# Bucketed attention and an MLP on one core: head pairs of the second pass transposed on TensorE instead of by DMA, four shared PSUM banks, scores in halves of 384 keys

## The chip, the core and the metric

The kernel runs on one core of a Trainium2 chip. A core has five engines with queues of their own: PE (TensorE, matrix products; its weight loads are listed as PEld), DVE (VectorE), ACT (ScalarE), POOL (GpSimd) and SP (SyncE, which here only issues DMA transfers). They share the on-chip memory SBUF (128 partitions); PE writes its products to PSUM, eight banks of 512 float32 words per partition, which DVE and ACT read and POOL does not touch in this kernel. The metric is the device time of one execution in microseconds, smaller is better.

## The reference, cut to what matters

The shapes are q, k, v of 4 batches x 8 heads x 768 rows x 64; proj is 64 x 6, w_in 512 x 2048, w_out 2048 x 512.

```python
q_bits = (np.einsum('bhsd,dk->bhsk', q, proj) > 0)      # k_bits alike
mask = q_bucket[:, :, :, None] == k_bucket[:, :, None, :]
scores = scale * np.matmul(q, k.transpose(0, 1, 3, 2))
scores = np.where(mask, scores, -1000000000.0)
attn = softmax(scores)                                  # minus the row's maximum; sum + 1e-9
x = np.matmul(attn, v)                                  # heads side by side: 3072 x 512
h = x @ w_in
out = (0.5 * h * (1.0 + erf(h / sqrt(2)))) @ w_out
```

A query sees only the keys whose six sign bits (the bucket) equal its own.

## The kernel before

**Number forms.** The MLP's products and most of the weighted sums of V are made of float16 halves: a number is written as a high and a low float16, and a product as three (high-high, high-low, low-high). Scores and hash are made in a 4-byte reduced form (`fp32r`), q and k each as a rounded part (tiles Aq, Ak) and a rest (Bq, Bk). The bits of query and key sit in extra rows of Aq and Ak, so that the score product itself lowers every pair of different buckets by a large number.

**A unit** is one head's 128 queries against all 768 keys; there are 192. `unit` (L688) plans it: the score product on PE (L697, L698) into a double bank `s`; the row's maximum on DVE (L701); two tiny DVE instructions (L705, L710); the exponential with its sum on ACT (L713) into `p`; a reciprocal (L722). Then the weights must be turned, keys to partitions, for the sum over V. That is done in one of two ways:

- *In halves* (all passes but the first): the weights times the reciprocal are written as a high float16 half `hl` on ACT, DVE or POOL (`affine`, L376 or L379), the low half by DVE (L728), and one transposing DMA turns both into `pt` (L735). The sum over V (L828) is then 36 float16 products for a pair of heads and 256 queries (a pair-chunk). V itself is split too (`values_halves`, L583).
- *Whole* (the first pass): a diagonal matrix `dr` with the reciprocals is made (L376/L379), PE multiplies the float32 weights with it, six 128x128 products that both scale and turn (L769, `whole_turn`), into two banks, and ACT or DVE copies each bank's 384 words to `pt`. The sum over V is 12 float32 products (L819), each of which leaves two records in the trace.

**Heads.** `head` (L594) loads a head's q and k, rounds them (Aq), moves halves (by DMA or an engine), subtracts for the rests (L398), makes the hash on PE (L659 to L664), its sign on ACT (L667), and the mask rows.

**Passes.** Pass one: batch 0, the first 256 queries of all eight heads (16 units). Pass two: batch 0, the other 512 queries in two chunks of 256, heads in reverse order (32 units). Then batches 1 to 3 with 48 units each. The number `cl` (0 for pass one, 1 for pass two, 2 after) chooses a pass's parameters and, before the change, whether weights are turned whole.

**The MLP** follows behind for each chunk of 256 rows, in two groups: the hidden layer (L1006) into `hp` banks, ACT copies it scaled (L1016), GELU, a split into halves `g` (one buffer), the output product (L1073), which adds up over both groups in the two banks `acc`, and a drain by DVE (L1093). The weights w_in and w_out are loaded, decoded by three integer instructions of DVE for each half (L452, L457, L462), scaled and split during passes one and two. The first output product waits for all of w_out.

**What sets the order.** The class `Plan` simulates the engines with a cost for every step, and each engine's queue is written in the order in which the simulation started its steps; ready steps of an engine compete by a key, which is the unit's number plus an offset from the table `PAR`. A step that can run on several engines takes the one that is free first. MLP steps have late keys (1000 and more) and so fill PE where attention leaves it free. Buffers are rings: a step that takes one waits until it is free. PSUM has the rings `s` (2 of two banks), `hp` (2 banks: hash, hidden layer, sum over V, weight statistics) and `acc` (2 banks: output sums, and under the name `turn` the whole turns of pass one).

Of the kernel before, what the change touches and what calls it, by code (L numbers as in the profile page):

```python
# [26 lines left out]
KEEP = 3  # L27
TABLE = 1.3
# [3 lines left out]
PAR = dict(H0=180.41, HL=-26.83, VS=-317.44, G2=1.83, HQ=-29.88, VQ=-3.01, in0=-31.49, out0=593.98, in1=111.61, out1=-36.62, in2=-95.35, out2=88.33, in3=-121.74, out3=193.55, H1=83.9, H2=30.05, H3=-106.39, H4=-26.07, H5=122.48, H6=11.83, H7=-6.57, MEV=-10, MGE=-10, MSP=-9, V0=74.23, QK0=76.28, QK1=22.19, QK2=79.24, MX0=-14.69, MX1=-2, MX2=67.11, EX0=-26.96, EX1=10.58, EX2=76.78, NR0=8.86, NR1=-1.85, NR2=92.39, HI0=-6.87, HI1=-39, HI2=-59.82, LO0=-16.45, LO1=50.99, LO2=34.82, PV0=94.26, PV1=48.91, PV2=24.55, TR0=-62.99, TR1=24.83, TR2=-50.58, V1=-109.62, V2=-89.25, Sin0=21.37, Sin1=-27.13, Sin2=50.05, Sin3=-25.72, Sout0=1.71, Sout1=35.63, Sout2=78.23, Sout3=-107.51, Lin=-90.3, Pin=-5.44, Qin=-44.82, Cin=-51.27, Min=-30.56, Lout=-67.78, Pout=75.58, Qout=-91.18, Cout=-17.92, Mout=204.75, G0=-24.93, G1=-27.5, G3=22.31, G4=-43.56, G5=-42.96, G6=-61.41, G7=2.72, DUP0=-47.65, DUP1=-23.1, DUP2=29.36, LOW0=-18.36, LOW1=24.39, LOW2=11.14, PRJ0=-0.65, PRJ1=-0.28, PRJ2=89.76, MSK0=66.33, MSK1=-99.41, MSK2=63.64, DI_ACT=-97.24, DI_DVE=-5.22, DI_Pool=0, WS_ACT=59.06, WS_DVE=0, WS_Pool=0, WH_ACT=-0.64, WH_DVE=0, WH_Pool=0, WL_ACT=0, WL_DVE=0.39, WL_Pool=0, VH_ACT=-74.31, VH_DVE=0.03, VH_Pool=0, MV_SP=0, MV_ACT=0, MV_DVE=0, MV_Pool=0, LO_ACT=0, LO_DVE=-37.1, LO_Pool=-1.97, RND_ACT=-0.17, RND_DVE=0, RND_Pool=0, MSK_ACT=-5.39, MSK_DVE=0, MSK_Pool=0, HI_ACT=-44.01, HI_DVE=0, HI_Pool=-3.05, DG_ACT=0.26, DG_DVE=0, DG_Pool=12.19, EV_ACT=0, EV_DVE=15.46, EV_Pool=0, GH_ACT=82.19, GH_DVE=-7.55, GH_Pool=52.8)  # L32
# [18 lines left out]
class Plan:  # L51
# [13 lines left out]
    START = {"DVE": 9.8, "Pool": 1.3, "SP": 0.7, "ACT": 3.7}  # L65
# [149 lines left out]
def tile_bucket_attention_moe(  # L215
# [33 lines left out]
        "s": 2, "hp": 2, "acc": 2, "p": 2, "hl": 2, "raw": 1, "rawe": RAWE, "sign": 1, "dr": 2, "turn": 2, "pt": NTH + 1,  # L249
# [5 lines left out]
    def ring(pool, name, shape, dtype, count, first=0):  # L255
# [48 lines left out]
    bufs["dr"] = ring(early, "dr", [P, P], F32, rings["dr"])  # L304
    bufs["turn"] = bufs["acc"]
# [15 lines left out]

    ident = const.tile([P, P], BF16, tag="ident", name="ident")
# [5 lines left out]
    off = const.tile([P, 1], F32, tag="off", name="off")  # L328
    nc.scalar.dma_start(out=off, in_=offset)
    praw = const.tile([P, 2 * NBIT], F32, tag="praw", name="praw")  # L330
    nc.scalar.dma_start(out=praw[:D, :NBIT], in_=proj)
    nc.scalar.dma_start(out=praw[D:, :NBIT], in_=proj)

    hash_hi = const.tile([P, D + P], F32R, tag="hash_hi", name="hash_hi")
    hash_lo = const.tile([P, P], F32R, tag="hash_lo", name="hash_lo")
    nc.vector.memset(hash_hi.bitcast(F32), 0.0)
    nc.vector.memset(hash_lo.bitcast(F32), 0.0)
    nc.vector.tensor_scalar(
        out=praw[:, NBIT:], in0=praw[:, :NBIT], scalar1=-1.0, scalar2=None, op0=ALU.mult
    )  # L340
    nc.vector.tensor_copy(out=hash_hi[:, D : D + 2 * NBIT], in_=praw)
    for rr in (slice(0, D), slice(D, P)):
        nc.vector.tensor_tensor(
            out=hash_lo[rr, rr.start : rr.start + 2 * NBIT], in0=praw[rr],
            in1=hash_hi[rr, D : D + 2 * NBIT].bitcast(F32), op=ALU.subtract,
        )
# [59 lines left out]
    def everywhere(t, top, key):  # L406
# [16 lines left out]
        return sc  # L423

# [169 lines left out]
    def head(b, h, i, key, clear, qr, cl):  # L594
# [57 lines left out]
        for c0, c1 in ((0, TC), (TC, S)):  # L652
# [4 lines left out]
            def project(n=n, box=box, with_q=with_q):  # L657
                pp = buf(box[0])[:, : n.stop - n.start]
                nc.tensor.matmul(pp, hash_lo, aq[:, n], start=True, stop=False)  # L659
# [12 lines left out]
            box.append(add("PE", 0.05 + (0.42e-3 * (2 + with_q)) * (c1 - c0), project, key + PAR[f"PRJ{cl}"], [space], takes="hp"))  # L672
# [15 lines left out]
    def unit(t, i, q0, qs, cl, made, place):  # L688
# [4 lines left out]

        def scores():
            for lo in range(0, S, 512):
                n = slice(lo, min(lo + 512, S))
                nc.tensor.matmul(buf(sp)[:, n], aq[:, qs], ak[:, n], start=True, stop=False)  # L697
                nc.tensor.matmul(buf(sp)[:, n], bq[:, qs.start - q0 : qs.stop - q0], bk[:, n], start=False, stop=True)  # L698
# [50 lines left out]
        if not cl:  # L749
            return sp, whole_turn(ex, nr, r, place, t)  # L750
# [9 lines left out]
    def whole_turn(ex, nr, r, place, t):  # L760
# [20 lines left out]
        dg = add(affine_on("DG", P, True), 0, diagonal, t + PAR["HI0"], [nr], takes="dr", port=True)  # L781
        prods, copies = [], []
        for n, (k0, k1) in enumerate(((0, KT // 2), (KT // 2, KT))):
            step = []
            step.append(
                add("PE", 0.214 * (k1 - k0), lambda k0=k0, k1=k1, step=step: product(k0, k1, step), t + PAR["LO0"], [dg], takes="turn")
# [4 lines left out]
                t + PAR["TR0"], [step[0], *hold[:1]], takes=None if hold else "pt",  # L791
# [10 lines left out]
    def values(b, pr, ch, vhl, turns, holds, key):  # L802
# [8 lines left out]

        whole = (b, ch) == (0, FIRST[0][0])
# [23 lines left out]
        for n, kt in enumerate(range(0, KT, 2)):  # L836
# [3 lines left out]
                    "PE", (0.9 if whole else 0.8) * nt / TC, lambda kts=kts: product(kts), key, [vh, vl, xt[b, ch], *turns, *parts],  # L840
# [311 lines left out]
```

## Time and profile before

| | |
|---|---|
| median of 3 runs | 972.09 us (970.51 to 973.16) |
| profiled execution | 971.92 us, span 970.1 us |
| PE busy | 874.6 us |
| DVE busy | 740.0 us |
| ACT busy | 640.9 us |
| POOL busy | 288.8 us |
| mean granted PE clock | 0.957 |

The busy time of an engine is the time in which it has an instruction running, as a sum over the span. In the rows of groups stand the line, engine, operation, output and inputs, shapes and count, then the busy time in us, the mean of one in ns, and the idle time before them with what ended it. The granted clock is the share of full speed at which PE was allowed to run.

### The profile page before, as it was taken

What the parts mean: (1) busy time and instruction counts of PE and PEld (TensorE: products, weight loads), DVE (VectorE), ACT (ScalarE), POOL (GpSimd) and SP (SyncE); (2) the same over time, 40 slices, a digit from 0 to 9 for tenths busy, and PEclk for the clock granted to TensorE, in tenths of its full rate; (3) what the DMA queues carried; (4) which work ended last, traced back from release to release, by engine and by line L of the source; (5) the groups of instructions that cost most, each with busy time, mean ns of one, the idle gap of its engine ahead of it and who ended that gap; (6) DMA issues with size and microseconds to landing.
All of it is one profiled execution on the core that took longest, in us unless ns stands there. A gap on an engine that the chain in (4) does not pass through costs nothing.

```text
span 970.1 us, 17419 instructions
## 1 busy us (share of the span) xinstructions
PE 874.6 (90%) x6512; PEld 630.8 (65%) x6512; DVE 740.0 (76%) x1607; ACT 640.9 (66%) x997; POOL 288.8 (30%) x241
## 2 busy tenths in 40 slices
PE   3768877556899999999999999999999999999998
PEld 2556666334576766867776676776776776667763
DVE  7888799999998879998897998998988842232222
ACT  4686788676868867888777778878878633112220
POOL 2565642722533224343232222423344100000000
PEclk9999888786799999999999999999999999999999
DMA  8654369786888778968677889876887830000000
GB/s 236 188 184 131 91 134 219 162 196 150 175 167 162 153 117 215 181 141 153 144 143 125 164 179 168 160 156 137 188 139 142 153 67 22 1 22 23 1 22 22
DMA packets 337124, 129.33 MB, mean 133 GB/s; under 512 B 278736, under 2 KB 322768, under 8 KB 337040
## 3 DMA queue, kind: packets, MB, share of 16 engines
q1 hardware_dynamic: 336736, 128.22, 62.6%
q8 instruction: 51, 0.84, 0.4%
q14 instruction: 33, 0.27, 0.1%
q10 hardware_dynamic: 304, 0.00, 0.0%
HBM read 45.49 MB, written 6.29 MB: 53 GB/s over the span
## 4 chain that ended last, share of the span: by engine, by line
PE 46%; DVE 14%; ACT 8%; DMA 7%; issue 4%; POOL 0%; SPq 0%; ACTq 0%; POOLq 0%; DVEq 0%
PE acc L1073 18%; PE hp L1006 16%; DMA pt<-hl 5%; PE hp L828 4%; PE s L697 4%; DVE rows L701 3%; PE s L698 3%; DVE hl L728 3%; ACT p L713 2%; DVE wraw L728 2%; DMA pt<-wraw 1%; DVE g L1054 1%; ACT h L1040 1%; ACT hl L376 1%; ACT L713 1%
## 5 line engine op out<-in xcount | busy, mean ns | idle before, releaser
L1006 PE MATMUL hp<-x,Win 128*128 128x256 f16 x2304 | 269.4, 274 | 0.4 <-ACT sign L667 0.4
L1073 PE MATMUL acc<-Wout,g 128*128 128x512 f16 x1152 | 261.0, 380 | 0.0
L1006 PEld LDWEIGHTS <-Win 128*128 128x128 f16 x2304 | 220.6, 98 | 35.1 <-issue 4.1
L701 DVE TENSOR_REDUCE rows<-s 128x1 f32<-128x768 f32 x192 | 179.8, 950 | 18.7 <-PE s L698 17.3
L1073 PEld LDWEIGHTS <-g 128*128 128x128 f16 x1152 | 108.0, 98 | 126.0 <-issue 5.1
L713 ACT ACTIVATE p<-s,rows 128x768 f32<-128x768 f32 x142 | 140.1, 987 | 45.1 <-DVE rows L710 17.0
L697 PE MATMUL s<-Ak,Aq 128*128 128x512 f32 x352 | 141.4, 404 | 27.4 <-ACT p L713 21.2
L1016 ACT ACTIVATE h<-hp,ffs 128x512 f32<-128x512 f32 x96 | 65.6, 683 | 133.2 <-PE hp L1006 132.8
L698 PE MATMUL s<-Bk,Bq 128*128 128x512 f32 x352 | 117.2, 353 | 0.0
L379 DVE TENSOR_SCALAR g<-h,ffs 128x512 f16<-128x512 f32 x48 | 25.0, 524 | 110.7 <-ACT h L1040 80.8
L697 PEld LDWEIGHTS s<-Ak,Aq 128*128 128x128 f32 x352 | 70.3, 200 | 60.0 <-ACT p L713 33.1
L728 DVE SCALAR_TENSOR_TENSOR hl<-p,rows,hl 128x768 f16<-128x768 f32 x95 | 103.3, 1095 | 7.2 <-ACT hl L376 6.2
L828 PE MATMUL hp<-pt,vhl 128*64 128x256 f16 x1584 | 100.8, 281 | 0.2 <-DVE x L855 0.2
L828 PEld LDWEIGHTS <-vhl 128*64 128x64 f16 x1584 | 84.7, 113 | 13.5 <-issue 7.8
L1054 DVE SCALAR_TENSOR_TENSOR g<-h,ffs,g 128x512 f16<-128x512 f32 x96 | 77.7, 816 | 14.6 <-ACT g L376 9.5
L698 PEld LDWEIGHTS s<-Bk,Bq 128*128 128x128 f32 x352 | 71.1, 202 | 9.7
L376 ACT ACTIVATE hl<-p,rows 128x768 f16<-128x768 f32 x53 | 49.1, 930 | 28.7 <-DMA pt<-hl 22.5
L667 ACT ACTIVATE sign<-hp,off 128x256 f32<-128x256 f32 (+1 forms) x74 | 42.0, 576 | 19.5 <-PE hp L664 19.0
L713 ACT ACTIVATE wraw<-s,rows 128x768 f32<-128x768 f32 x50 | 49.3, 986 | 7.2 <-DVE rows L710 4.5
L398 POOL TENSOR_TENSOR Bq<-raw,Aq 64x768 fp32r<-64x768 f32 (+1 forms) x22 | 41.2, 1871 | 39.6 <-ACT Aq L376 25.1
L379 POOL TENSOR_SCALAR hl<-p,rows 128x768 f16<-128x768 f32 x28 | 30.9, 1102 | 64.4 <-DVE rows L722 21.4
L1040 ACT ACTIVATE h<-h 128x2048 f32<-128x2048 f32 x24 | 45.9, 1911 | 0.4
(154 smaller groups left out, 1211.1 us busy)
## 6 DMA issues: line engine op xcount, KB each, us to landing
raw<-qk SPq DMA_DIRECT2D x29, 384.0 KB, 3.6
vraw<-v SPq DMA_DIRECT2D x28, 384.0 KB, 3.9
wraw<-w_in SPq DMA_DIRECT2D x16, 512.0 KB, 4.4
wraw<-w_out SPq DMA_DIRECT2D x16, 512.0 KB, 5.1
out<-o SPq DMA_DIRECT2D x12, 512.0 KB, 3.0
rawe<-qk SPq DMA_DIRECT2D x8, 384.0 KB, 3.2
Ak<-Aq SPq DMA_DIRECT2D x13, 192.0 KB, 4.0
Bk<-Aq SPq DMA_DIRECT2D x12, 192.0 KB, 3.2
```

Of the source, the lines that this page charges most:

```text
L376: nc.scalar.activation(out=out, in_=in_, func=AF.Copy, scale=scale, bias=bias)
L379: on.tensor_scalar(out=out, in0=in_, scalar1=scale, scalar2=bias, op0=ALU.mult, op1=ALU.add)
L697: nc.tensor.matmul(buf(sp)[:, n], aq[:, qs], ak[:, n], start=True, stop=False)
L698: nc.tensor.matmul(buf(sp)[:, n], bq[:, qs.start - q0 : qs.stop - q0], bk[:, n], start=False, stop=True)
L701: nc.vector.tensor_reduce(out=nm, in_=buf(sp)[:, :S], axis=AX.X, op=ALU.max, negate=True)
L713: nc.scalar.activation(out=buf(ex), in_=buf(sp)[:, :S], func=AF.Exp, scale=sc, bias=nb, accum_out=ssum)
L728: nc.vector.scalar_tensor_tensor(out=buf(hi)[:, 1], in0=buf(ex), scalar=r, in1=buf(hi)[:, 0], op0=ALU.mult, op1=ALU.subtract,)
L828: nc.tensor.matmul(pv[j * D : (j + 1) * D], buf(vh)[:, tv, kt, j * D : (j + 1) * D], buf(holds[j][0])[:, tp * KT + kt, :nt], start=kt == 0 ...
L1006: nc.tensor.matmul(buf(pair[0])[:, j * ch[1] : (j + 1) * ch[1]], win_hl[:, f0 // WB1, tw, pr, f0 % WB1 : f0 % WB1 + P], x[:, tx, pr, : ch[1]],
L1016: nc.scalar.activation(out=bufs["h"][0][:, 2 * fp : 2 * fp + 2, :nt], in_=buf(pair[0])[:, : 2 * nt].rearrange("p (j k) -> p j k", j=2), fu ...
L1054: nc.vector.scalar_tensor_tensor(out=gt[:, 1, s2, :nt], in0=h[:, s2, :nt], scalar=sg, in1=gt[:, 0, s2, :nt], op0=ALU.mult, op1=ALU.subtract,)
L1073: nc.tensor.matmul(bufs["acc"][u].rearrange("p (c f) -> p c f", c=NWB), gt[:, tg, f, u * P : (u + 1) * P], wout_hl[:, :, tw, ft], start=ft ...
```

## The change

It does six things.

1. `WHOLE = (4, 3, 0, 0, 0)` says how many head pairs of each pass turn their weights whole. Pass one keeps its four; in pass two the first three of four now do, 24 units of 32; `whole` takes the place of `not cl` in `unit` and `values`.
2. The rings `hp`, `acc` and `turn` become one ring `hp` of four PSUM banks. A chunk's output sums take two of them from the moment when the first split of its `g` is done until their drain.
3. The score product is made in two halves of 384 keys, each in a PSUM bank of its own, instead of 512 and 256; the maximum and the exponential read both as one two-part access.
4. The hash operand is 44 columns wide instead of 128, the keys' bits start at row 32, and the sign tile has 64 rows.
5. At the start, proj is loaded first, by one transfer on ACT's queue and one on SP's, ahead of the first head; the offset comes in two small transfers; `ones` is cleared on POOL, and four of the five Ak tiles are cleared by steps of the plan, on DVE or POOL.
6. The table `PAR`, some costs and a start time of the plan have new numbers, so the order moves everywhere.

```diff
+WHOLE = (4, 3, 0, 0, 0)
...
-        "s": 2, "hp": 2, "acc": 2, "p": 2, "hl": 2, "raw": 1, "rawe": RAWE, "sign": 1, "dr": 2, "turn": 2, "pt": NTH + 1,
+        "s": 2, "hp": 4, "p": 2, "hl": 2, "raw": 1, "rawe": RAWE, "sign": 1, "dr": 2, "pt": NTH + 1,
...
+    nc.scalar.dma_start(out=praw[:D, :NBIT], in_=proj)
+    nc.sync.dma_start(out=praw[D:, :NBIT], in_=proj)
...
-    nc.vector.memset(ones, 1.0)
-    for _, ak, _, _ in sets:
-        nc.vector.memset(ak[D:].bitcast(F32), 0.0)
...
+    nc.gpsimd.memset(ones, 1.0)
...
+    nc.vector.memset(sets[0][1][D:].bitcast(F32), 0.0)
...
+    cleared = {}
+    for n, (_, ak, _, _) in enumerate(sets[1:]):
+        box = []
+
+        def clear(ak=ak, box=box):
+            on = nc.vector if box[0].engine == "DVE" else nc.gpsimd
+            on.memset(ak[D:].bitcast(F32), 0.0)
+
+        box.append(add({"DVE": (0.7, 0.0), "Pool": (0.85, 0.0)}, 0, clear, n + PAR["Z"]))
+        cleared[n + 1] = box
...
+        def both(step):
+
+            return buf(step).rearrange("p (b k) -> p b k", b=2)[:, :, : S // 2]
+
         def scores():
-            for lo in range(0, S, 512):
-                n = slice(lo, min(lo + 512, S))
...
+            for half in range(2):
+                n = slice(half * S // 2, (half + 1) * S // 2)
+                to = both(sp)[:, half]
...
-        if not cl:
-            return sp, whole_turn(ex, nr, r, place, t)
+        if whole:
+            return sp, whole_turn(ex, nr, r, place, cl, t)
...
-                add("PE", 0.214 * (k1 - k0), lambda k0=k0, k1=k1, step=step: product(k0, k1, step), t + PAR["LO0"], [dg], takes="turn")
+                add("PE", 0.214 * (k1 - k0), lambda k0=k0, k1=k1, step=step: product(k0, k1, step), t + PAR[f"LO{cl}"], [dg], takes="hp")
...
-        whole = (b, ch) == (0, FIRST[0][0])
...
-                vhl = values_halves(b, pr, key, v_ready[b]) if cl else values_whole(b, pr, key)
+                whole = pos // 2 < WHOLE[n_pass]
+                vhl = values_whole(b, pr, key) if whole else values_halves(b, pr, key, v_ready[b])
...
+            banks = [add("none", 0, lambda: None, LATE + n, [cur["split"][0][1]], takes="hp") for u in range(nt // P)]
...
-            needs = [*cur["split"][f // 2], *acc[-1:]]
+            needs = [*cur["split"][f // 2], *acc[-1:], *banks]
             if g == 0 and f == 0:
-                needs += out_w if n == 0 else [drained]
+                needs += out_w if n == 0 else []
...
+            for bank in banks:
+                free(bank, [drained])
```

Counted over the whole program, the order has 240 of the 128x128 products with a diagonal instead of 96 (each a pair of records), 101 transposing transfers instead of 125, 152 low halves of weights on DVE instead of 176, 13 of V instead of 16, and 80 copies of turned weights out of PSUM instead of 32, 42 of them on DVE and 38 on ACT.

The order moves at the following places. In the rows stand the line of the kernel that they belong to, the operation, and output and inputs; hp, s, p, dr, pt and the others are the tiles named above, with a buffer's number behind them.

PE in pass two, before the change, around the 34th unit: scores of one unit follow those of another, and the hash of a later head (hash_lo, hash_hi) stands between them.

```order
L697 MATMUL s_61<-Ak_91,Aq_90 128x512
L698 MATMUL s_61<-Bk_93,Bq_92 128x512
L697 MATMUL s_61<-Ak_91,Aq_90 128x256
L698 MATMUL s_61<-Bk_93,Bq_92 128x256
L659 MATMUL hp_64<-x_105,hash_lo 128x256
L664 MATMUL hp_64<-x_107,hash_hi 128x256
L697 MATMUL s_62<-Ak_91,Aq_90 128x512
L698 MATMUL s_62<-Bk_93,Bq_92 128x512
L697 MATMUL s_62<-Ak_91,Aq_90 128x256
L698 MATMUL s_62<-Bk_93,Bq_92 128x256
```

PE at about the same place with the change:

```order
L788 MATMUL hp_64<-dr_120,p_68 128x128 x3
L788 MATMUL hp_65<-dr_119,p_67 128x128 x3
L788 MATMUL hp_66<-dr_119,p_67 128x128 x3
L715 MATMUL s_62<-Ak_91,Aq_90 128x384
L716 MATMUL s_62<-Bk_93,Bq_92 128x384
L715 MATMUL s_62<-Ak_91,Aq_90 128x384
L716 MATMUL s_62<-Bk_93,Bq_92 128x384
```

Products with the diagonal, three to a bank, now stand between the scores of one unit and the next, and take turns on the same four banks as all else.

DVE in pass two, before the change, around the 39th unit:

```order
L701 TENSOR_REDUCE rows<-s_62 128x1
L701 TENSOR_REDUCE rows<-s_61 128x1
L705 TENSOR_SCALAR rows<-rows 128x1
L728 SCALAR_TENSOR_TENSOR hl_70<-p_68,rows,hl_70 128x768
L710 TENSOR_SCALAR rows<-rows 128x1
L705 TENSOR_SCALAR rows<-rows 128x1
L462 SCALAR_TENSOR_TENSOR Wout<-wraw_82,Wout 128x512
L710 TENSOR_SCALAR rows<-rows 128x1
L462 SCALAR_TENSOR_TENSOR Wout<-wraw_83,Wout 128x512
L728 SCALAR_TENSOR_TENSOR hl_69<-p_67,rows,hl_69 128x768
```

DVE at about the same place with the change:

```order
L470 SCALAR_TENSOR_TENSOR Wout<-wraw_82,Wout 128x512
L470 SCALAR_TENSOR_TENSOR Wout<-wraw_81,Wout 128x512
L719 TENSOR_REDUCE rows<-s_62 128x1
L380 TENSOR_SCALAR pt_73<-hp_65 128x3x128
L723 TENSOR_SCALAR rows<-rows 128x1
L380 TENSOR_SCALAR pt_73<-hp_64 128x3x128
L728 TENSOR_SCALAR rows<-rows 128x1
```

The low halves are gone from between the maxima and the decodes of w_out, and copies of 384 words out of PSUM stand there.

DVE at the start, before the change:

```order
L325 MEMSET ones 128x128
L327 MEMSET Ak_87 64x768
L327 MEMSET Ak_91 64x768
L327 MEMSET x_106 64x768
L327 MEMSET Ak_112 64x768
L327 MEMSET Ak_116 64x768
L336 MEMSET hash_hi 128x192
L337 MEMSET hash_lo 128x128
L338 TENSOR_SCALAR praw<-praw 128x6
L341 CAST hash_hi<-praw 128x12
```

DVE at the start, with the change:

```order
L336 MEMSET hash_hi 128x76
L337 MEMSET hash_lo 128x44
L338 MEMSET Ak_87 64x768
L339 TENSOR_SCALAR praw<-praw 128x6
L342 CAST hash_hi<-praw 128x12
L344 TENSOR_TENSOR hash_lo<-praw,hash_hi 64x12 x2
L399 TENSOR_TENSOR Bq_88<-rawe_121,Aq_86 64x256
L399 TENSOR_TENSOR Bk_89<-rawe_121,Aq_86 64x768
```

Five of DVE's clearing instructions went to POOL's queue, and the rests of the first head came onto DVE. The first output product stands behind the 55th unit's scores, where it stood behind the 53rd; the hidden layer of the first chunk, which stood between the 20th and the 31st unit, is spread from the 22nd to the 47th.

More of the change, by code (lines that the diff above doesn't have):

```diff
@@ L64 @@
     SAME = {"PE": 0.0, "DVE": 0.13}
-    START = {"DVE": 9.8, "Pool": 1.3, "SP": 0.7, "ACT": 3.7}
+    START = {"DVE": 4.6, "Pool": 1.3, "SP": 0.7, "ACT": 3.7}
     QUEUE = 2.0
@@ L319, in buf @@
         return bufs[step.takes][step.slot]
+    KR = 32
+    HR = KR + 2 * NBIT
+    praw = const.tile([P, 2 * NBIT], F32, tag="praw", name="praw")
+    nc.scalar.dma_start(out=praw[:D, :NBIT], in_=proj)
+    nc.sync.dma_start(out=praw[D:, :NBIT], in_=proj)
+    off = const.tile([2 * KR, 1], F32, tag="off", name="off")
+    for n in range(2):
+        nc.scalar.dma_start(out=off[n * KR : (n + 1) * KR], in_=offset[n * D : n * D + KR])
     ident = const.tile([P, P], BF16, tag="ident", name="ident")
@@ L324, in tile_bucket_attention_moe @@
     ones = const.tile([P, P], BF16, tag="ones", name="ones")
-    nc.vector.memset(ones, 1.0)
-    for _, ak, _, _ in sets:
-        nc.vector.memset(ak[D:].bitcast(F32), 0.0)
[L328 to L335, printed above, removed]
+    nc.gpsimd.memset(ones, 1.0)
+    hash_hi = const.tile([P, KR + HR], F32R, tag="hash_hi", name="hash_hi")
+    hash_lo = const.tile([P, HR], F32R, tag="hash_lo", name="hash_lo")
     nc.vector.memset(hash_hi.bitcast(F32), 0.0)
     nc.vector.memset(hash_lo.bitcast(F32), 0.0)
+    nc.vector.memset(sets[0][1][D:].bitcast(F32), 0.0)
     nc.vector.tensor_scalar(
@@ L340, in tile_bucket_attention_moe @@
     )
-    nc.vector.tensor_copy(out=hash_hi[:, D : D + 2 * NBIT], in_=praw)
-    for rr in (slice(0, D), slice(D, P)):
+    nc.vector.tensor_copy(out=hash_hi[:, KR : KR + 2 * NBIT], in_=praw)
+    for n, rr in enumerate((slice(0, D), slice(D, P))):
         nc.vector.tensor_tensor(
-            out=hash_lo[rr, rr.start : rr.start + 2 * NBIT], in0=praw[rr],
-            in1=hash_hi[rr, D : D + 2 * NBIT].bitcast(F32), op=ALU.subtract,
+            out=hash_lo[rr, n * KR : n * KR + 2 * NBIT], in0=praw[rr],
+            in1=hash_hi[rr, KR : KR + 2 * NBIT].bitcast(F32), op=ALU.subtract,
         )
@@ L686, in head, with unit @@
         return [m3, r1, r2]
-    def unit(t, i, q0, qs, cl, made, place):
+    def unit(t, i, q0, qs, cl, whole, made, place):
         aq, ak, bq, bk = sets[i]
@@ L738, in turn @@
             )
-        unity = 2.0**-15 if cl else 1.0
+        unity = 1.0 if whole else 2.0**-15
         si_on = SI[cl]
-        sp = add("PE", 0.66, scores, t - PAR[f"QK{cl}"], made, takes="s")
+        sp = add("PE", 0.78, scores, t - PAR[f"QK{cl}"], made, takes="s")
         mx = add("DVE", 0.87, top, t - PAR[f"MX{cl}"], [sp])
@@ L790, in whole_turn @@
                 lambda k0=k0, k1=k1, step=step: copy(step[1].engine, k0, k1, step),
-                t + PAR["TR0"], [step[0], *hold[:1]], takes=None if hold else "pt",
+                t + PAR[f"TR{cl}"], [step[0], *hold[:1]], takes=None if hold else "pt",
             )
@@ L800, in whole_turn, with values @@
         return copies
-    def values(b, pr, ch, vhl, turns, holds, key):
+    def values(b, pr, ch, whole, vhl, turns, holds, key):
         vh, vl = vhl
@@ L928, in tile_bucket_attention_moe @@
                     qs = slice(ch[0] + u * P, ch[0] + (u + 1) * P)
-                    sp, tr = unit(t, i, base, qs, cl, made, (holds[h % 2, ch], u))
+                    sp, tr = unit(t, i, base, qs, cl, whole, made, (holds[h % 2, ch], u))
                     uses.append(sp)
@@ L935, in tile_bucket_attention_moe @@
                         values(
-                            b, pr, ch, vhl, turns[0, ch] + turns[1, ch], [holds[0, ch], holds[1, ch]],
+                            b, pr, ch, whole, vhl, turns[0, ch] + turns[1, ch], [holds[0, ch], holds[1, ch]],
                             t + PAR[f"PV{cl}"],
```

53 lines of the change are left out of this document (26 added, 27 removed).

## The prediction

> **What bounds the kernel now.** I read the page first, then a table of 25 us stretches with the busy time of each engine, then the groups of equal instructions, then pieces of the order of time. The profiled execution took 971.92 us (span 970.1 us and 1.8 us around it); it stands 0.17 us under the median of the three runs, 972.09, so I sum against 971.9.
>
> ```profile
> span 970.1 us, 17419 instructions
> PE 874.6 (90%) x6512; PEld 630.8 (65%) x6512; DVE 740.0 (76%) x1607; ACT 640.9 (66%) x997; POOL 288.8 (30%) x241
> ...
> PE   3768877556899999999999999999999999999998
> ...
> DVE  7888799999998879998897998998988842232222
> ...
> PEclk9999888786799999999999999999999999999999
> ```
>
> PE (TensorE) is full from the twelfth slice (267 us) to the end, at full clock. Before that it has holes, and from the fifth to the eleventh slice the granted clock sinks too. So the time is PE's whole work plus what PE loses in the first 275 us. A change can win only there, or by taking work off PE; work added to PE costs its full price unless it falls into those holes.
>
> ```profile
> 75.00:100.00 25.00, 22.22 (x158) 17.01 (x154) 21.57 (x59) 15.73 (x37) 12.61 (x12) 0.93 0.42 122
> 100.00:125.00 25.00, 21.09 (x142) 16.33 (x142) 18.89 (x38) 20.72 (x36) 17.25 (x10) 0.86 0.50 113
> 125.00:150.00 25.00, 19.81 (x164) 15.77 (x161) 24.32 (x42) 21.04 (x32) 10.22 (x9) 0.86 0.63 131
> 150.00:175.00 25.00, 16.12 (x131) 12.39 (x128) 23.29 (x51) 21.40 (x34) 7.84 (x7) 0.84 1.05 223
> 175.00:200.00 25.00, 15.73 (x120) 11.00 (x118) 22.34 (x40) 17.90 (x31) 13.65 (x9) 0.82 0.72 158
> 200.00:225.00 25.00, 14.10 (x85) 10.12 (x87) 23.67 (x53) 17.26 (x30) 5.26 (x5) 0.73 0.97 222
> 225.00:250.00 25.00, 15.87 (x111) 12.15 (x111) 23.64 (x49) 18.05 (x33) 9.64 (x7) 0.64 0.62 139
> 250.00:275.00 25.00, 24.26 (x160) 15.71 (x159) 24.27 (x63) 18.77 (x32) 12.09 (x10) 0.89 0.78 162
> 275.00:300.00 25.00, 23.85 (x186) 18.07 (x185) 22.45 (x51) 18.18 (x28) 9.09 (x7) 1.00 0.92 176
> ...
> 400.00:500.00 100.00, 98.74 (x773) 71.59 (x770) 89.70 (x207) 83.30 (x125) 37.36 (x33) 1.00 0.79 153
> ```
>
> The columns are PE, PEld, DVE, ACT, POOL, granted clock, DMA share, GB/s. Pass two lies in 100 to 275 us. There PE is busy 127.0 of 175 us (sum of the seven rows); each row times its clock gives 103.7 us of full-clock work, a rate of 0.59. DVE is busy 160.4 us, 0.92: it is what the stage waits for. ACT stands at 135.1, 0.77.
>
> ```profile
> 249.41 2.77 POOL L398 TENSOR_TENSOR Wout<-o,Wout 128x1024 f16<-128x1024 f32 x1 [3.04 <-ACT Wout L376]
> ...
> L398 DVE TENSOR_TENSOR Wout<-o,Wout x1: 1215/1215/1215, 256.0 to 256.0; 128x1024 f16<-128x1024 f32 x1
> ...
> 257.94 2.76 PE L1073 MATMUL acc<-Wout,g 128*128 128x512 f16 x12
> ```
>
> The stage ends when the last piece of w_out is split: DVE's piece begins at 256.0, the first output product at 257.94. Until then PE has nothing of the MLP left but the first chunk's hidden layer. The decodes of w_out (L452, L457, L462) stand in DVE's queue between the attention's instructions, so DVE's load sets this end as well.
>
> **The change, part by part.** *Pass two, DVE.* 24 of 32 units lose the split into halves; three head pairs lose the split of V.
>
> ```profile
> L728 DVE SCALAR_TENSOR_TENSOR hl<-p,rows,hl 128x768 f16<-128x768 f32 x95 | 103.3, 1095 | 7.2 <-ACT hl L376 6.2 <-POOL hl L379 0.7
> ...
> L376 ACT ACTIVATE hl<-p,rows 128x768 f16<-128x768 f32 x53 | 49.1, 930 | 28.7 <-DMA pt<-hl 22.5 <-DVE rows L705 4.0 <-DVE rows L722 1.9
> ...
> L583 DVE SCALAR_TENSOR_TENSOR vhl<-vraw,s_v,vhl 128x768 f16<-128x768 f32 x16 | 17.5, 1092 | 0.0
> ...
> L379 DVE TENSOR_SCALAR hl<-p,rows 128x768 f16<-128x768 f32 x14 | 12.7, 905 | 2.3 <-DMA pt<-hl 1.9
> ...
> L376 ACT ACTIVATE pt<-acc 128x384 f32<-128x384 f32 x17 | 8.3, 489 | 8.9 <-PE acc L769 8.6 <-DVE rows L705 0.2
> L379 DVE TENSOR_SCALAR pt<-acc 128x384 f32<-128x384 f32 x15 | 8.3, 553 | 3.2 <-PE acc L769 3.0
> ...
> L376 ACT ACTIVATE dr<-ident,rows 128x128 f32<-128x128 bf16 x10 | 4.0, 397 | 3.5 <-DVE rows L722 3.3
> ...
> L379 DVE TENSOR_SCALAR dr<-ident,rows 128x128 f32<-128x128 bf16 x2 | 1.9, 950 | 0.0
> ```
>
> DVE loses 24 low halves at 1.095 (26.3 us), 3 of V at 1.092 (3.3) and, by the order's counts up to the 53rd unit, 5 high halves at 0.905 (4.5). It gains 27 of the 48 copies out of PSUM at 0.553 (14.9) and 2 diagonals at 0.950 (1.9). Net -17.3: 143.1 us remain in the stage. ACT takes the other 21 copies at 0.489 (10.3) and 13 diagonals at 0.397 (5.2), and by the same counts gives up 11 high halves of p at 0.930 (10.2) and smaller work; it stays about as full and never was the limit.
>
> *Pass two, PE.* Added: 144 float32 products with a diagonal, each two records in the trace; and in six pair-chunks the weighted sum of V as 24 float32 records instead of 36 of f16.
>
> ```profile
> 62.39 1.50 PE L769 MATMUL acc<-dr,p 128*128 128x128 f32 x12
> 63.73 0.62 PE L475 MATMUL hp<-Win 128*128 128x128 bf16 x8
> ...
> L769 PE MATMUL acc<-dr,p 128*128 128x128 f32 x192 | 27.1, 294 | 5.9 <-ACT dr L376 5.3 <-ACT pt L376 0.5
> ...
> L828 PE MATMUL hp<-pt,vhl 128*64 128x256 f16 x1584 | 100.8, 281 | 0.2 <-DVE x L855 0.2
> ...
> L819 PE MATMUL hp<-pt,vhl 128*64 128x256 f32 x96 | 13.6, 425 | 3.3 <-DVE tiny L416 2.9 <-DVE inv L365 0.4
> ...
> 103.72 2.81 PE L819 MATMUL hp<-pt,vhl 128*64 128x256 f32 x24
> ```
>
> Six products took 1.34 us from start to the next start (0.22 each), or 27.1/96 = 0.28 by the group, which holds cold stretches: 32 to 41 us, taken 36 (0.25, six in the 1.50 that the row itself shows). V: 24 records in 2.81, or 3.4 by the group's mean, for 36 at 2.29 (100.8/1584 x 36): +0.5 to +1.1 a chunk, taken +0.5, 3 us in six. PE gains 39 us (35 to 48), so 103.7 becomes 143 us of full-clock work.
>
> So both engines now need 143 us in a stage that took 175. DVE at its old 0.92 would give 156. PE's rate was 0.83 in the stretch 75 to 100 (22.22 x 0.93 / 25), which is this very kind of work with PE transposes, and 0.95 in 275 to 300: 173 and 150. What hides the 39 us is PE's 48 us of holes and the 23 us that the low clock costs (127.0 - 103.7); without that cover it would all be paid. I take 165, at which both run at 0.87, between the two rows of PE: **-10**, ends -19 and -2. Waits are added: each product needs a free PSUM bank and the diagonal, and the next unit's scores stand behind it on PE, on which DVE's maximum waits. Each bank comes free with its copy, half a microsecond on ACT or DVE; that, and not DVE's sum, is why I don't take 156.
>
> *DMA.* 24 of 125 transposing transfers go. In 150 to 175 and 200 to 225 us the DMA share is 1.05 and 0.97; the idle time of 22.5 us before ACT's high halves hangs on these transfers, over the whole span. No further term: it is part of what lets DVE keep its rate.
>
> *The start.*
>
> ```profile
> 8.19 1.29 DVE L338 TENSOR_SCALAR praw<-praw 128x6 f32<-128x6 f32 x1 [2.62 <-DMA praw<-proj]
> ...
> 10.22 0.55 PE L659 MATMUL hp<-Aq,hash_lo 128*128 128x256 f32 x1 [10.22 <-DVE hash_lo L343]
> ```
>
> The first product waited for the hash operand, that for proj, which now is loaded first, on two queues. The first head's load stands one issue later on SP's queue. The Ak memsets leave DVE for POOL, ahead of POOL's first move of a half; DVE takes the first head's low halves instead. The end between no gain and the 2.62 us wait plus a like time in the mask's step, 5 us: taken **-2**.
>
> *At nothing.* The scores keep 1536 moving columns in four matmuls:
>
> ```profile
> 61.70 0.40 PE L697 MATMUL s<-Ak,Aq 128*128 128x512 f32 x1
> 61.93 0.39 PE L698 MATMUL s<-Bk,Bq 128*128 128x512 f32 x1
> 62.16 0.28 PE L697 MATMUL s<-Ak,Aq 128*128 128x256 f32 x1
> 62.27 0.28 PE L698 MATMUL s<-Bk,Bq 128*128 128x256 f32 x1
> ```
>
> Start to start they take 0.23, 0.23, 0.11 and 0.12, in step with their columns, so four of 384 take 0.69 again; I allow 2 us over 192 units either way. The narrow hash operand moves the same columns. The four shared PSUM banks: from 400 to 500 us PE idles 1.3 us, so at most some 6 us are to be won in 300 to 750. To be lost is a wait at each of 11 chunk changes, while the old and the new chunk's sums hold all four banks, for the first bank's drain:
>
> ```profile
> L1093 DVE TENSOR_TENSOR o<-acc,ffs 128x512 f32<-128x512 f32 x24 | 15.4, 683 | 8.6 <-PE acc L1073 8.6
> ```
>
> 11 times 0.68 is 8 us. Taken 0.
>
> Sum: 971.9 - 10 - 2 = 959.9, **960 us**; own range 952 to 968.
>
> **The rivals.** *PE becomes the bound of pass two* (slower). Between the 0.73 of 100 to 125 us (21.09 x 0.86 / 25) and the 0.83 above lies 0.78: 143/0.78 = 183 us, +8, with the start 978. For it: PE's order is fixed, and every unit now crosses from PE to DVE to ACT, back to PE and out again. Against: DVE, not PE, was full. It decides from a PE rate below 0.82 (143/175).
>
> *The clock stays down* (slower). Its mean over PE's busy time in the stage is 103.7/127.0 = 0.82; if it stayed, 143 becomes 175 us of busy time, and at a busy share of 0.95 the stage takes 184: +9, with the start 979. Against it: the stretch 75 to 100 us, full of such products, had 0.93. The Trainium skill (TensorE: Matmul & The Clock Gate, section Part 4: PE-mode transpose) says that transposes in TensorE's transpose mode don't count as busy for the clock; by that rule this rival would hold. The trace speaks against it here, since these are ordinary products with a diagonal.
>
> *DVE alone decides*: 156 us, 971.9 - 19 - 2 = 951. For it: the hidden layer of the first chunk (192 products) is now spread through the pass as filler.
>
> *No difference*: w_out's loads, POOL's splits (2.77) and the single buffer of g fix the end at 258 us whatever DVE does; only the start's 2 us come: 970. Against: the decodes wait in DVE's own queue.
>
> **How the numbers follow.** Forecast 0.47, DVE alone 0.17, no difference 0.13, PE bound 0.18, clock 0.05. About 0.3%, 2.9 us, is what a measurement here can tell from no change. Faster: 0.47 and 0.17 and a little of the third, 0.66; same 0.13; slower 0.21. The range reaches into both outer cases and takes in the banks' cost: 945 to 979.
>
> **What would show it.** Right: the first output product comes at 244 to 250 us instead of 257.94, the clock between 150 and 250 us is above 0.9, DVE's busy time up to there is some 20 us less, and from there on PE is as full as before. Wrong: PE's full-clock rate in the pass below 0.82 with waits for PSUM copies ahead of L788, or new idle time of PE after 300 us at the chunk changes.

## The result, and the profile after

| | before | after |
|---|---|---|
| median | 972.62 us (4 runs) | 945.70 us (944.65 to 947.56, 4 runs) |
| profiled execution (span) | 971.92 (970.1) | 945.44 (943.6) |
| PE busy | 874.6 us | 888.9 us |
| DVE busy | 740.0 us | 723.4 us |
| ACT busy | 640.9 us | 606.7 us |
| mean granted PE clock | 0.957 | 0.981 |

The ratio is 0.9736, 95% interval 0.9712 to 0.9759: 26.9 us faster, where 12 had been forecast. The page of the changed kernel, its busy tenths in 40 slices:

```profile
span 943.6 us, 17819 instructions
PE 888.9 (94%) x6728; PEld 643.4 (68%) x6728; DVE 723.4 (77%) x1601; ACT 606.7 (64%) x972; POOL 316.4 (34%) x279
...
PE   4779999966999999999999999999999999999998
...
PEclk8999999987999999999999999999999999999999
```

Most of PE's holes between 75 and 200 us are filled, and the clock stays up there. The same stretches as in the prediction (PE, PEld, DVE, ACT, POOL, granted clock, DMA share, GB/s):

```profile
100.00:125.00 25.00, 23.90 (x181) 19.29 (x182) 19.16 (x52) 22.63 (x46) 20.99 (x16) 1.00 0.27 77
125.00:150.00 25.00, 24.95 (x208) 21.67 (x205) 23.81 (x54) 19.88 (x43) 12.04 (x11) 1.00 0.60 171
150.00:175.00 25.00, 24.95 (x239) 21.08 (x237) 23.68 (x64) 21.08 (x44) 9.71 (x9) 1.00 0.57 162
175.00:200.00 25.00, 21.85 (x172) 16.40 (x169) 22.87 (x45) 19.23 (x29) 17.12 (x13) 0.93 0.52 137
200.00:225.00 25.00, 15.86 (x110) 12.40 (x107) 19.54 (x44) 21.94 (x36) 10.41 (x8) 0.73 0.54 110
225.00:250.00 25.00, 19.86 (x148) 13.25 (x148) 23.98 (x52) 17.52 (x27) 10.55 (x9) 0.93 0.71 149
250.00:275.00 25.00, 24.47 (x186) 17.96 (x185) 23.02 (x54) 17.36 (x29) 12.49 (x10) 1.00 0.81 159
```

From 125 to 175 us PE runs without a pause at full clock while DVE is 95% busy. One large hole is left, in 200 to 225 us. Over the whole of 100 to 275 us PE does 148.6 us of full-clock work (each row's busy time times its clock), a rate of 0.85 where it had been 0.59. The first output product has moved from 257.94 to 239.71 us:

```profile
239.71 2.76 PE L1092 MATMUL hp<-Wout,g 128*128 128x512 f16 x12
```

The groups that the change enlarges, columns as before:

```profile
L788 PE MATMUL hp<-dr,p 128*128 128x128 f32 x480 | 66.0, 292 | 4.2 <-ACT dr L377 2.3 <-ACT pt L377 1.3 <-DVE dr L380 0.5
L836 PE MATMUL hp<-pt,vhl 128*64 128x256 f32 x240 | 29.0, 385 | 0.4 <-DVE rows L723 0.4
...
L380 DVE TENSOR_SCALAR pt<-hp 128x384 f32<-128x384 f32 x42 | 22.9, 552 | 3.8 <-PE hp L788 3.1 <-ACT Win L377 0.2
...
L747 DVE SCALAR_TENSOR_TENSOR hl<-p,rows,hl 128x768 f16<-128x768 f32 x73 | 76.4, 1051 | 2.6 <-POOL hl L380 1.6 <-ACT hl L377 0.6
```

A copy costs 0.552 us, as before. For a product the group gives 66.0/240 = 0.275 us, but that is too much: a group's busy time runs to the end of the last record of each stretch, and by then the next instruction has begun. Three products between two others:

```profile
137.18 0.83 PE L788 MATMUL hp<-dr,p 128*128 128x128 f32 x6
137.85 2.78 PE L1024 MATMUL hp<-x,Win 128*128 128x256 f16 x24
```

They are busy for 0.83 us, but the next product starts after 0.67, so each takes 0.22 us of PE's time, the lower end of the prediction's bounds.

**An account that helps to read all runs.** In each 5 us of a trace I take PE's *loss*: the time that passed less PE's busy time times the granted clock. What is left of the span is PE's *work* at full clock. Work plus loss is the span, so each run's time can be told in these two.

| profiled run | span | work | loss to 100 us | 100 to 300 | 300 to end | first output product at |
|---|---|---|---|---|---|---|
| before | 970.1 | 845.4 | 36.7 | 73.3 | 14.8 | 257.9 |
| after | 943.6 | 876.7 | 30.5 | 25.8 | 10.7 | 239.7 |
| no whole turns in pass two, searched (e1) | 972.5 | 847.3 | 36.5 | 73.3 | 15.5 | 247.6 |
| before, searched (e13) | 973.3 | 844.1 | 38.3 | 78.4 | 12.5 | 265.0 |
| before + whole turns, old table (e2) | 969.1 | 886.2 | 33.2 | 34.8 | 14.8 | 260.6 |
| before + whole turns, searched (e9) | 938.5 | 875.7 | 35.5 | 18.1 | 9.3 | 239.7 |
| after, DVE's lows again (e6) | 972.2 | 883.1 | 30.0 | 48.0 | 11.1 | 267.5 |
| after, products twice (e5) | 973.0 | 909.1 | 29.5 | 23.8 | 10.6 | 269.2 |

The change added 31.3 us of work and took away 57.8 us of loss: 47.5 in 100 to 300 us, 6.2 before, 4.1 behind. The difference, 26.5, is the gain of the profiled run. (Work is known only to some 5 us: the runs with the same added instructions lie between 874 and 886. If each PE record is counted from its start to the next one's start, or to its own end where that comes first, times the granted clock, the widest spread between these runs is in the score products, 153.1 to 162.8 us; why is not settled.)

### The profile page after: what moved, and what is told of

Same layout as the page of the kernel before. It is cut to its first block, busy times and chain, and to the rows that moved or that the text cites. A ratio compares the mean times of both kernels' runs of the same rounds, so it can differ in the third digit from the quotient of the medians.

```text
span 943.6 us, 17819 instructions
## 1 busy us (share of the span) xinstructions
PE 888.9 (94%) x6728; PEld 643.4 (68%) x6728; DVE 723.4 (77%) x1601; ACT 606.7 (64%) x972; POOL 316.4 (34%) x279
## 5 line engine op out<-in xcount | busy, mean ns | idle before, releaser
L1092 PE MATMUL hp<-Wout,g 128*128 128x512 f16 x1152 | 260.9, 380 | 0.0
L715 PE MATMUL s<-Ak,Aq 128*128 128x384 f32 x352 | 139.4, 396 | 24.1 <-ACT p L731 14.0
L716 PE MATMUL s<-Bk,Bq 128*128 128x384 f32 x352 | 120.9, 343 | 0.0
L380 DVE TENSOR_SCALAR g<-h,ffs 128x512 f16<-128x512 f32 x36 | 20.3, 563 | 118.9 <-ACT h L1058 84.4
L380 POOL TENSOR_SCALAR g<-h,ffs 128x512 f16<-128x512 f32 x36 | 30.5, 848 | 207.6 <-PE hp L1092 152.1
L845 PE MATMUL hp<-pt,vhl 128*64 128x256 f16 x1368 | 84.1, 275 | 1.1 <-DMA pt<-hl 0.9
L747 DVE SCALAR_TENSOR_TENSOR hl<-p,rows,hl 128x768 f16<-128x768 f32 x73 | 76.4, 1051 | 2.6 <-POOL hl L380 1.6
L788 PE MATMUL hp<-dr,p 128*128 128x128 f32 x480 | 66.0, 292 | 4.2 <-ACT dr L377 2.3
L788 PEld LDWEIGHTS hp<-dr,p 128*128 128x128 f32 x480 | 61.8, 204 | 8.2 <-ACT dr L377 3.2
L680 ACT ACTIVATE sign<-hp,off 44x256 f32<-44x256 f32 (+1 forms) x74 | 41.7, 571 | 24.7 <-PE hp L677 21.4
L399 POOL TENSOR_TENSOR Bq<-raw,Aq 64x768 fp32r<-64x768 f32 x23 | 42.6, 1852 | 41.9 <-ACT Aq L377 18.1
```

Of the source, the lines that this page charges most:

```text
L380: on.tensor_scalar(out=out, in0=in_, scalar1=scale, scalar2=bias, op0=ALU.mult, op1=ALU.add)
L715: nc.tensor.matmul(to, aq[:, qs], ak[:, n], start=True, stop=False)
L716: nc.tensor.matmul(to, bq[:, qs.start - q0 : qs.stop - q0], bk[:, n], start=False, stop=True)
L747: nc.vector.scalar_tensor_tensor(out=buf(hi)[:, 1], in0=buf(ex), scalar=r, in1=buf(hi)[:, 0], op0=ALU.mult, op1=ALU.subtract,)
L788: nc.tensor.matmul(buf(step[0])[:, (k - k0) * P : (k - k0 + 1) * P], buf(ex)[:, words(k)], buf(dg), start=True, stop=True,)
L845: nc.tensor.matmul(pv[j * D : (j + 1) * D], buf(vh)[:, tv, kt, j * D : (j + 1) * D], buf(holds[j][0])[:, tp * KT + kt, :nt], start=kt == 0 ...
```

## The experiments

Two theories at first. **A**: the whole turns are the gain, DVE is freed and PE's holes take the products. **B**: the whole turns are worth the forecast's 10 us, and the shared banks and the new order are most of it. Because the order comes from a simulation steered by the table `PAR`, a part that is undone leaves a table made for something else. So in several runs the table was *searched*: its entries were changed at random for the same time in each case, keeping what shortened the plan's own simulated order. No time of a search is used here, only the chip's.

**e1: pass two in halves again, all else of the change kept, table searched.**

```diff
-WHOLE = (4, 3, 0, 0, 0)
+WHOLE = (4, 0, 0, 0, 0)
```

> The changed kernel with only pass one turned whole: pass two splits its weights and uses transposing DMA again, all else of the change stays, and the table of keys is searched anew for it. Theory A (the whole turns in pass two are the gain: DVE is freed and PE's holes take the products): the time goes back to 965 to 975. Theory B (the four shared banks and the new order are most of it, the whole turns are worth the 10 us that were forecast): 953 to 960.

Measured 973.77 us, ratio to before 1.0011 (0.9989 to 1.0033): the whole gain is gone. Theory B falls in its first half: shared banks, halves of 384, early loads and a searched order give nothing together without the whole turns, in the one order that was searched for them.

**e2: the kernel before with whole turns in pass two and nothing else.** The same lines of `unit`, `whole_turn` and `values` as in the change; banks, start and table stay as before.

> The kernel before, its table of keys untouched, with the whole turns for three pairs of pass two added and nothing else (banks apart, old start, 512 and 256 keys). Theory A: 948 to 958, most of the 27 us. Theory B: 960 to 968.

Measured 973.39 us, ratio 1.0010 (0.9990 to 1.0029). A miss for both theories: the whole turns alone give nothing either. Attention did run ahead: the 53rd unit's maximum stood at 239.6 us, before the change at 258.3. But the first output product came at 260.6, because w_out was not ready. The instructions that touch w_out from 225 us on, durations as least/median/most, then first and last start:

```profile
L463 DVE SCALAR_TENSOR_TENSOR Wout<-wraw,Wout x2: 683/687/691, 224.4 to 226.6; 128x512 int32<-128x512 int32 x2
L377 ACT ACTIVATE o<-Wout,tiny x2: 1137/1138/1138, 247.8 to 255.8; 128x1024 f32<-128x1024 f32 x2
L399 POOL TENSOR_TENSOR Wout<-o,Wout x2: 2131/2424/2716, 252.2 to 258.1; 128x1024 f16<-128x1024 f32 x2
```

DVE's decode was done at 227 us; what was left of the scaling on ACT began 21 us later, behind attention's instructions in ACT's queue. PE is full from 100 to 175 us in this run (74.98 of 75 us, at a clock of 1.00); later its rows are:

```profile
225.00:250.00 25.00, 16.73 (x144) 12.97 (x144) 23.69 (x67) 19.52 (x34) 6.10 (x5) 0.84 0.69 137
250.00:275.00 25.00, 20.04 (x102) 12.73 (x102) 23.60 (x51) 20.31 (x33) 14.42 (x10) 0.77 0.65 136
```

The holes that the products filled up to 175 us open again here. In the account: work +40.8, loss -41.8. The products were paid exactly by holes, and nothing was left over.

**e3 and e10: the changed kernel with the banks apart, as before, two searches of the table.**

```diff
-        "s": 2, "hp": 4, "p": 2, "hl": 2, ...
+        "s": 2, "hp": 2, "acc": 2, "turn": 2, "p": 2, "hl": 2, ...
...
```

> The changed kernel with two banks for hp and two for output sums and turns, as before, and the table searched anew for it. Theory A: within 5 us of the changed kernel, 941 to 951. Theory B: 955 to 965.

> The changed kernel with banks apart, a second search of its table from another seed. If sharing is worth 15 to 20 us whatever the order: 955 to 965, as the first (959.38). If the first search was only unlucky: 942 to 950.

**e4 and e11: the changed kernel itself, two searches of its table.**

> The changed kernel with nothing changed but its table of keys, searched as long as the tables of the two runs with parts undone, so that these are compared with an equal. Both theories: not slower than the changed kernel, 930 to 946.

> The changed kernel, a second search of its table from another seed. If shared banks carry the difference: 936 to 946, as the first (940.44). If the first was lucky: 946 to 958.

Measured: apart 959.38 and 953.61, shared 940.44 (0.9661, 0.9619 to 0.9703) and 945.15. 953.61 lies between the two ranges that were expected for it. That looked like 8 to 19 us for sharing, a point for the rest of theory B. But e4 and e11 differ by 5 us with the same program and only another order, and e9 below took the reading back.

**e9 and e14: the kernel before with whole turns, as e2, and only the table searched; two searches.** Banks apart, old start, 512 and 256 keys.

> The kernel before with three pairs of pass two turned whole, banks apart and the old start, and its table of keys searched anew. With the untouched table it gained nothing (973.39): attention ran 25 us ahead, but w_out's split and the MLP stood where they were. If the order was what was missing: 953 to 962, like the changed kernel with banks apart (959.38). If the whole turns need the shared banks: 968 to 975.

> The kernel before with three pairs of pass two turned whole, banks apart, a second search of its table from another seed. If whole turns and an order made for them suffice: 935 to 948. If the first was lucky: 955 to 965.

Measured 938.23 us, ratio 0.9660 (0.9631 to 0.9690), and 956.49 us, ratio 0.9840 (0.9810 to 0.9871). The first lies below both of its ranges, the second in the range for a lucky first. e9 is e2 with other numbers in the table, which set the order and, for steps that can run on several engines, the engine: 35 us less, faster than the changed kernel and with none of its other parts. Its first output product stands at 239.7 us, not 260.6:

```profile
225.00:250.00 25.00, 21.77 (x172) 15.37 (x171) 23.23 (x53) 22.87 (x35) 20.00 (x14) 1.00 0.71 135
250.00:275.00 25.00, 24.46 (x192) 18.73 (x191) 19.98 (x45) 20.05 (x29) 5.97 (x6) 1.00 0.81 147
```

The hole of e2 is closed: ACT and POOL, idle there in e2 for part of the time, do the scaling of w_out earlier (the last one on ACT starts at 223.8 us instead of 255.8). That is not all: of the 30.6 us between the two profiled runs, 16.7 are loss from 100 to 300 us, 10.5 are work. And the time of the first output product alone does not order the runs. In e3 it stands at 219.8 us with the scores of 45 units ahead of it, in e14 at 238.2 with 48, in e9 at 239.7 with 54, and e9 is the fastest. In e10 it stands at 238.1 with 53, almost as in e9; there the loss from 300 us on (16.9 for 9.3) and the work (883.6 for 875.7) make the 15 us between them.

**e13: the kernel before, only its table searched.**

> The kernel before with nothing changed but its table of keys, searched as long as the others. If the order alone is worth something: 950 to 965. If whole turns are what gives the order room: 966 to 975.

Measured 972.84 us, ratio 1.0016 (0.9993 to 1.0038). The search alone gives nothing. With e1 that makes two searched orders without whole turns in pass two, and neither gains, while each searched order with them, in every run here, gains 12 us or more.

**e15: e9's kernel with the four banks shared, searched.**

> The same with the four banks shared and its table searched. If sharing is worth 10 to 19 us, as the runs on the changed kernel seemed to say: 920 to 930. If it is worth nothing with an order made for banks apart: 934 to 946.

Measured 946.62 us, ratio 0.9737 (0.9704 to 0.9769), just above the range for no worth. With whole turns and banks apart there are now four orders, 938.23, 953.61, 956.49 and 959.38; with shared banks four, 940.44, 945.15, 945.70 and 946.62. The means are 951.9 and 944.5, but orders of one kind differ by up to 21 us. The fastest has banks apart. So sharing is not needed for the gain, and whether it is worth some 7 us in the mean stays open.

**e12: all four pairs of pass two turned whole, searched.**

```diff
-WHOLE = (4, 3, 0, 0, 0)
+WHOLE = (4, 4, 0, 0, 0)
```

> The changed kernel with all four pairs of pass two turned whole, its table searched anew. The fourth pair adds 48 products, about 13 us of PE work, and takes 8 low halves (8.4 us) from DVE. If DVE still bounds the pass: 932 to 940. If PE's work now counts in full: 946 to 956.

Measured 949.71 us, ratio 0.9790 (0.9755 to 0.9825), 5 to 9 us more than the like-searched three pairs; the expectation's DVE side missed. From 100 to 300 us PE lost only 5.3 us in it; e4 and e11 with three pairs had lost only 8.0 and 6.0 there, so there were hardly any holes left for 48 more products.

**e5 and e6: the changed kernel's order kept, one engine loaded more in pass two.** e5 issues each product of pass two twice into the same place; e6 lets DVE compute the 24 low halves into a spare tile.

```diff
-            for k in range(k0, k1):
+            for k in [*range(k0, k1)] * (2 if cl == 1 else 1):
```

```diff
...
             nc.vector.reciprocal(out=r, in_=si)
+            if whole and cl == 1:
+                nc.vector.scalar_tensor_tensor(
+                    out=spare, in0=buf(ex), scalar=r, in1=spare, op0=ALU.mult, op1=ALU.subtract
+                )
```

> The changed kernel with every product with the diagonal in pass two issued twice (144 more, about 39 us of PE work by the changed kernel's own 66.0 us for 240), the order untouched otherwise. If PE is now the bound of pass two (its rate from 100 to 175 us was 0.98): 30 to 40 us are paid, 975 to 987. If DVE still is, holes take most of it: 948 to 960.

> The changed kernel with DVE's 24 low halves of pass two computed again into a spare tile that nobody reads (24 x 1.05 = 25 us of DVE), nothing else of the halves. If DVE bounds pass two: 15 to 25 us more, 960 to 971. If PE does: under 8, 946 to 954.

Measured 974.57 and 971.67 us: +28.9 and +26.0 against the changed kernel, each 0.4 to 0.7 us outside the range expected for an engine that bounds. The products' group in e5, and the added group in e6:

```profile
L788 PE MATMUL hp<-dr,p 128*128 128x128 f32 x768 | 97.9, 285 | 4.1 <-ACT dr L377 2.2 <-ACT pt L377 1.2 <-ACT p L731 0.7
```

```profile
L745 DVE SCALAR_TENSOR_TENSOR spare<-p,rows,spare 128x768 f16<-128x768 f32 x24 | 28.5, 1188 | 0.9
```

28.5 us of DVE cost 26.0. The 144 products more are 31.9 us of PE (97.9 instead of 66.0), 0.22 each and not the 39 us in all that was expected; they cost 28.9. One stretch of e5, then of e6, beside the changed kernel's above:

```profile
125.00:150.00 25.00, 25.00 (x205) 22.53 (x202) 16.56 (x37) 16.32 (x33) 12.99 (x10) 1.00 0.28 83
```

```profile
125.00:150.00 25.00, 20.07 (x131) 16.67 (x130) 24.14 (x44) 16.22 (x33) 15.04 (x11) 0.86 0.29 82
```

More PE work starves DVE (16.56 for 23.81), more DVE work starves PE (20.07 for 24.95). I had put the two runs as alternatives, and both came out on the paying side: in this order both engines are at the limit at once. Without the relief of DVE, 24 low halves, and with PE's products kept, the whole gain is gone. e6 keeps the other reliefs, the fewer transposing transfers and the high halves that are gone, so these alone don't carry the gain in this order. Whether DVE's relief alone would carry it was not run, nor an order searched for the heavier load.

**e7: scores in 512 and 256 keys again, every instruction in its place.** The maximum and the exponential read one part again.

```diff
-            for half in range(2):
-                n = slice(half * S // 2, (half + 1) * S // 2)
-                to = both(sp)[:, half]
+            for lo in range(0, S, 512):
+                n = slice(lo, min(lo + 512, S))
+                to = buf(sp)[:, n]
...
```

> The changed kernel with scores in 512 and 256 keys again, every other instruction in the same place. If the halves cost nothing, as forecast: within 2 us of the changed kernel. If weight loads hide better behind 384 columns than behind 256, or the second bank helps: 3 to 10 us slower.

Measured 945.52 us, ratio 0.9728 (0.9702 to 0.9754): nothing, as forecast.

**e8: proj behind the offset on ACT's queue again, order untouched. e16: e9 with the early loads.**

```diff
-    nc.scalar.dma_start(out=praw[:D, :NBIT], in_=proj)
-    nc.sync.dma_start(out=praw[D:, :NBIT], in_=proj)
...
+    nc.scalar.dma_start(out=praw[:D, :NBIT], in_=proj)
+    nc.scalar.dma_start(out=praw[D:, :NBIT], in_=proj)
```

> The changed kernel with proj loaded on ACT's queue behind the offset again, as before the change; nothing else moved. If the early loads are worth the 2 us that the first scores came earlier: 946 to 949. If the start is hidden by what follows: within 1 us of the changed kernel.

> The first of the searched kernels with whole turns and banks apart (938.23), with proj loaded first on two queues. If the 3.7 us measured on the changed kernel add up: 933 to 937. If the start is hidden here, since five memsets still stand ahead of it on DVE: 937 to 940.

e8 measured 949.39 us, ratio 0.9768 (0.9743 to 0.9792): 3.7 us more by the medians, though the intervals of the two ratios overlap and the two profiled runs differ by 1.9 us only. Its first maximum stands at 15.4 us again, as before the change (13.2 with it). e16 measured 937.14 us, ratio 0.9640 (0.9607 to 0.9674), against 0.9660 for e9: within the uncertainty. Some 2 to 4 us in the changed kernel is likely, none is shown in e9's. e16 has the lowest median of all runs here, with banks apart and scores of 512 and 256.

## Why the prediction was wrong

**What bounds the kernel: right.** PE's work plus its loss is the time, and the loss lay in the first 300 us. Read by this account, the prediction implied 39 us of work and 51 us of loss recovered, 49 in pass two and 2 at the start; the trace shows 31.3 and 57.8. In 100 to 300 us the loss fell by 47.5 us, close to the 49. So the part of the mechanism by which holes and sunken clock pay the products held. The 14.5 us between the forecast's 12 and the 26.5 of the profiled run lie in two terms: the added work was priced about 8 us too high, and the time outside the pass fell by about 8 us more than the sum allowed; the 1.5 us less of loss recovered in the pass go against them.

**1. "PE gains 39 us": mis-sized, 31.3 by the account.** I took 0.25 us for a product, 36 us for 144. A product takes 0.22 us to the next start, and e5's 144 more are 31.9 us: my lower bound of 32 was right. The group's mean in the trace before, 0.28, from which I had the upper bound, counts the overlap with the next instruction too. Counted by the time to the next start at the granted clock, the products with the diagonal rose by 32.0 us (23.2 to 55.2) and the sum over V by 4.4 (104.8 to 109.2, for my 3). The rest of PE's work fell by about 4 us, mostly the hash products, 48.5 to 43.8. This account is good to some 5 us, so the size of this term is less certain than its sign.

**2. Everything outside the pass at 2 us: mis-sized, 10.3.** The loss fell by 6.2 us before 100 us and by 4.1 behind 300. The start's own -2 was about right: the first maximum came 2.2 us earlier, e8 says some 3.7. What I left at nothing was pass one's later half: the 16th unit's maximum stood at 84.4 us for 91.8, in e8 without the early loads at 87.6. So some 4 of these 7.4 us are not the start. They seem to belong to this order rather than to a part of the change: in the same program with other tables that maximum stood at 83.3 (e4) and 90.3 us (e11). For the 4.1 us behind 300 us the cause stays open; the loss there ranges from 9.3 (e9) to 22.4 us (e3).

**3. Pass two, "I take 165": the rate was near, partly by luck.** 143 us of work in 165 is a rate of 0.87; PE's was 0.85 from 100 to 275 us. It came about otherwise than I argued. From 125 to 175 us PE ran at (24.95 + 24.95)/50 = 1.00 with DVE at 0.95, beyond my upper row of 0.95, and in the hole at 200 to 225 us it did 15.86 x 0.73 = 11.6 us of work in 25. My reason for not taking 156, the wait for a bank's copy, showed as 1.3 us of waiting for ACT's copies in all. The pass gained 16.2 us (47.5 less 31.3) and not 10 because less work was added, not because PE ran faster than I took. The first output product came 18.2 us earlier, which looks like the rival in which DVE alone decides (-19), but 7.4 of them had come by the 16th unit's maximum; from there it was 166.1 us before and 155.3 after, 10.8 less. In this time two more units' scores and one more pair-chunk of V are done, 2 x 0.69 + 2.29 = 3.7 us by the prediction's own prices. The document had said that the first output product stands behind the 55th unit instead of the 53rd, and I never put it into the sum.

Of the signs that I had named, the granted clock was 1.00, 0.93, 0.73 and 0.93 between 150 and 250 us and so above 0.9 only outside the hole; DVE's busy time up to the first output product fell from 224.6 to 208.5 us, 16 for the 20; the first output product came before the 244 to 250 that I gave.

**The end of the stage: the argument was wrong, and the luck good.** I wrote that the decodes stand in DVE's queue, so that DVE's load sets the end, against the rival "no difference". e2 is that rival come true: DVE freed, decode done at 227 us, and still the first output product at 260.6, because w_out's scaling stood behind attention in ACT's queue and POOL's splits waited for it. What overcomes it is a table made for the whole turns (the change's sixth item), which I treated as a shuffle without a price: between e2 and e9, which differ in nothing else, it is worth 35 us, between e2 and e14 17. That the time fell all the same is luck as far as my argument goes.

**At nothing.** The halves of 384: right (e7). The narrow hash operand, which "moves the same columns": not tried alone, and perhaps not nothing. By the time to the next start at the granted clock the hash products take 46.5 to 48.6 us in the seven runs with the wide operand and 43.4 to 46.0 in the eleven with the narrow one. The shared banks, taken 0 between -6 and +8: not settled, -7 in the mean of four orders each.

**The other rivals.** *PE becomes the bound*: it does from 125 to 175 us, at a rate of 1.00, and over 100 to 275 us at 0.85 rather than 0.78, so that the time fell. *The clock stays down*: it rose to 1.00 in the stretches full of products, which speaks against applying the Trainium skill's sentence on transposes (TensorE: Matmul & The Clock Gate, Part 4: PE-mode transpose) to products with a diagonal. From 100 us on it fell to 0.73 in the hole at 200 to 225 us and to 0.93 in the stretches beside it.

## What to carry to other kernels

When one engine is full from some point on, account for a change as that engine's work plus its loss, stage by stage: moving work onto it gains only if more loss goes than work comes. Freeing another engine does not close the holes by itself; look for what the next stage waits for and whether the order brings it forward (here the scaling of w_out; the hole before it was some 17 of the 30.6 us between e2 and e9). And where an order is searched, one order is one sample: the same program ranged over 18 us between two searched orders here, and over 35 us if the old table is counted, so a part should be credited only over several orders, or with the order kept.

## What the runs showed of the hardware that was not expected

The transfer of 1.5 KB for proj landed 5.7 us after its issue when it was issued beside the first large loads, and in 2 us when issued ahead of them. The issues up to 30 us, before and then after, with the median us to landing last:

```profile
praw<-proj ACTq DMA_DIRECT2D x2, 1.5 KB, 5.7
```

```profile
praw<-proj SPq DMA_DIRECT2D x1, 1.5 KB, 2.2
praw<-proj ACTq DMA_DIRECT2D x1, 1.5 KB, 1.9
```

In e8, with proj behind the offset again, it landed in 5.8 us. The first instruction that used it took 1.29 us before and 0.56 after, but 0.17 in e8, so its length doesn't follow from when proj lands. After, then e8:

```profile
3.03 0.56 DVE L339 TENSOR_SCALAR praw<-praw 128x6 f32<-128x6 f32 x1 [1.13 <-DMA praw<-proj]
```

```profile
8.66 0.17 DVE L339 TENSOR_SCALAR praw<-praw 128x6 f32<-128x6 f32 x1 [6.76 <-DMA praw<-proj]
```

From 125 to 175 us of the changed kernel, PE was busy 49.90 of 50 us at a granted clock of 1.00 while f16, 4-byte and float32 products followed one another, and in e2 74.98 of 75 us from 100 to 175; I had not expected more than 0.95 there.
